# Score products with token slices as the stationary operand in an attention and mixture kernel

## The chip, the cores and the metric

One Trainium2 chip, one of its cores. The metric is the device time of one execution in microseconds (us). A run is one execution; the kernel before was timed in three, and one further execution was profiled. The engines are TensorE (PE in the profile; PEld is its weight load), VectorE (DVE), ScalarE (ACT), GpSimd (POOL) and SyncE (SP), which issues the large transfers. SBUF is the working memory of 128 partitions, PSUM the small memory of eight banks into which TensorE writes.

## What is computed

The agents attend to the keys, the queries attend to the agents, and the result x goes through a soft mixture of eight small networks with four slots each. There are 4 batches of 11456 tokens with 128 channels, 49 agents, and 32 slots in all. Everything is float32.

```python
def sm(a, b):                                   # softmax over b
    s = scale * (a @ b.transpose(0, 2, 1))
    e = np.exp(s - s.max(-1, keepdims=True))
    return e / (e.sum(-1, keepdims=True) + 1e-09)

agent_v = sm(agents, k) @ v                     # 4 x 49 x 128
x = (sm(q, agents) @ agent_v).reshape(45824, 128)

logits = x @ phi                                # 45824 x 32
d = softmax over the tokens (axis 0) of logits
c = softmax over the slots (axis 1) of logits
slot_input = d.T @ x                            # 32 x 128
slot_out[e] = np.maximum(slot_input[e] @ w1[e], 0.0) @ w2[e]
out = c @ slot_out
```

## The kernel before

**Tiling.** A batch has 90 cells of 128 tokens. A group is 16 cells (the last of a batch 10), so there are 24 groups of keys and 24 of queries. The x of the reference is never formed: the weights of the queries over the agents (`pt`) are multiplied with the agents' values times phi (`bd_m`), which gives the logits at once, and the sums over the tokens (`gp`) are taken of `pt`, too.

**Scores.** A batch is laid out as four streams of tokens (line 23). `scores` (line 227) makes four matmuls for each half h of the agents: the stationary operand is 32 agents (64 with padding), the moving one a stream's 512 tokens, and each stream's result goes to its own 32 partitions of a PSUM bank (tag "s", four banks). So the agents come out on partitions and the tokens along the row. Four matmuls with outputs on four strips of 32 partitions run side by side in the array; most float32 matmuls leave two records in the trace.

**Keys** (`k_ops`, line 239). `kx` and `kv` load a group; `ks` makes both halves of scores; `km` takes the maximum along the row (line 262); `kt`, `kr`, `kb`, `kn` carry the running maximum across the partitions through small matmuls into a bias per partition; `ke` (line 289) takes the exponential straight from PSUM with that bias. Then the tokens have to come to the partitions: `kT` transposes on VectorE in blocks of 32 x 32 (line 300), in group 0 on TensorE (`kP`, `kQ`). `kE` (line 318) multiplies with the values, two cells side by side on 64 partitions each; `kA` adds to the accumulator. At a batch's end `kg` and `kh` make `av` and `bd_m`.

**Queries** (`q_ops`, line 411). `qx` loads, `qs` makes scores, `qt` transposes them on VectorE into `pt` (line 434), `qm` takes the maximum over the 49 agents of each token (line 439). The exponential is made in one of two ways: for the even of the first 19 groups cell by cell on ScalarE with bias and accumulated sum (`qE`, line 460; `qw_act` on GpSimd), for the others with a subtraction on GpSimd (`qu`, line 444) and one exponential (`qe`, line 450; among the first 19 the sum is taken on VectorE, `qw_dve`, line 469). `qp` transposes `pt` on TensorE (line 504), `qc` copies it back, `ql` makes the logits: in the first 19 groups with the slots on partitions (line 481), which are transposed on VectorE (`qv`, line 490) and normalised on GpSimd (`qg`); in the last five with the tokens on partitions (line 517), normalised on VectorE (`qn`, lines 527 to 529). `qM` takes the column maximum over cells (line 536), `cr`, `cu`, `ce` the row softmax into `x_all`.

**Rounds** (`r_ops`, line 605). One or two groups make a round, 13 in all: `r1` to `r5` bring the column maximum to all partitions, `ru`, `re`, `rm` make the weighted exponentials `dt` (GpSimd, ScalarE, GpSimd; the multiplication of rounds 11 and 12 on VectorE, line 651), and `rg` sums `dt` x `pt` on TensorE (line 660: 32 columns stationary, 50 moving, four strips).

**End.** `z_` functions join the rounds and normalise, `m_` functions run the eight networks, `os`, `om`, `ot` (lines 872 to 889) normalise the first chunks of `x_all`, `fl` (line 891) are matmuls of no use to the result. The output loop (line 1016) makes 24 chunks with a matmul, two copies and a transfer each.

**Order.** Each engine runs its instructions in the order in which they are emitted. That order is the text `ORDER` (lines 47 to 104), which lists the steps of all groups interleaved; `_order` checks that each step stands behind what it needs, `_slots` gives the buffers in that order. `BUFS` (line 105) has the number of buffers: two `kt`, three `vt` and `qt`, four "s", three "a", one "m". The costs beside each step (`o("km", ..., 100 + 31 * n, ...)`) are notes for whoever makes the order; nothing on the chip reads them. The transfers of keys, values and queries all go through SP's queue, in the text's order, and each waits there for its buffer.

Of the kernel before, what the change touches and what calls it, by code (L numbers as in the profile page):

```python
# [16 lines left out]
S = E * SE  # L17
P = 128
# [7 lines left out]
NG = len(GROUPS)  # L26
EPS = 1e-9
# [20 lines left out]
qx qx qs.0 qs.1 qx qt.0 qs.0 qt.1 qm kx qs.1 qE.0 qt.0 qE.1 qs.0 qt.1 kv qm qs.1 qE.2 qt.0 qp.0  # L48
qu ks.0 qE.3 qt.1 ks.1 kx qm qe qp.1 km.0 qc.0 qp.0 qw@0 km.1 qc.1 qp.1 qc.0 qr kt qw@1 qE.0 kv
kr qr ks.0 qE.1 kb ks.1 km.0 kn ke.0 kx qp.0 km.1 ke.1 kP.0 qE.2 kt kr kb kT.0 kn ka kP.1 kx  # L50
qE.3 ks.0 kT.1 ke.0 ks.1 km.0 ke.1 kT.0 qp.1 kv qc.1 km.1 qw@2 qc.0 kE kT.1 qc.1 qr kx kt ks.0
kA kr kb kE km.0 kn ka ke.0 ke.1 kT.0 kv kT.1 ks.1 kA ks.0 km.1 kt kE km.0 kx kr kb kv ks.1 kA
kn ka ke.0 km.1 ke.1 ks.0 kT.0 kt ks.1 kr kT.1 kx kb kn km.0 ka kE ke.0 km.1 ke.1 kT.0 kT.1 kt
kv kr kE kA qx kb ks.0 kA kn ka ke.0 ks.1 ke.1 km.0 kT.0 km.1 kv kT.1 kt qs.0 kr kb kE qt.0 kn
ke.0 kx ke.1 kT.0 qs.1 kA kT.1 kg.2 qt.1 kg.1 kE kh.1 kh.2 qm kh.4 kv qu kg.3 kA ks.0 kh.3 ks.1
km.0 qe qx ql.0 km.1 ql.1 qn.0 kt ql.0 qn.1 kr qg ql.1 qn.0 kb kx qp.0 qn.1 kn ka qM qp.1 ke.0
qg qs.0 cr ke.1 qM cu qc.0 qs.1 qt.0 qc.1 ql.0 ce r1 kv qt.1 ql.1 qn.0 qm ks.0 kT.0 r2 qE.0
# [1052 lines left out]
```

## Time and profile before

| | us |
|---|---|
| three runs | 335.11, 337.64, 340.8 |
| median | 337.64 |
| the profiled execution | 333.75 |
| its span, first to last instruction | 332.0 |

The span is the time from the first to the last instruction of the profiled execution; the execution's own time is 1.75 us longer. Lines of the profile show, for an instruction or a group of them: the line of the kernel, the engine, the operation, what it writes and reads (tile names without buffer numbers), the shapes as partitions x elements, and a count. In the groups, the numbers behind the bar are busy time in us and the mean of one in ns, then the engine's idle time before them and what ended it. In the order of time, the first number is the start and the second the length in us. In the stretches, each engine has its busy us and its number of instructions, then come TensorE's granted clock, the busy share of the transfer engines and GB/s. Busy time of one engine can overlap at its ends, above all TensorE's, whose ends are modelled.

### The profile page before, as it was taken

The numbers are of one execution on the slowest core, as the hardware profiler recorded it, in microseconds if no ns is written. First come the engines' busy times: TensorE is split into PE (matmuls) and PEld (weight loads), VectorE is DVE, ScalarE is ACT, GpSimd is POOL, SyncE is SP. The second block draws the span as 40 slices with busy tenths as digits, with TensorE's granted clock in tenths as the row PEclk, the third lists the DMA queues.
The fourth block names the chain that finished last, engine by engine and source line by source line (L and its number), as shares of the span: only waits on it lengthen the run. The fifth ranks groups of instructions, "written<-read, shape, count | busy, mean of one in ns | idle before, by whom it ended". The sixth has DMA issues, their size and how long they took to land.

```text
span 332.0 us, 9455 instructions
## 1 busy us (share of the span) xinstructions
PE 274.5 (83%) x3821; PEld 152.7 (46%) x3821; DVE 264.7 (80%) x580; ACT 195.7 (59%) x613; POOL 139.8 (42%) x158
## 2 busy tenths in 40 slices
PE   1978978988998989898999989998978885866740
PEld 0234455544554455365556447467765551121210
DVE  0754675989998898999998988999949649998830
ACT  2496333484979685686956986374442246655540
POOL 0100001418382454638236938566886205343400
PEclk9999999999999999999999999999968999678555
DMA  7999899999979649989839990699400019999996
GB/s 298 423 409 359 319 395 418 421 410 402 393 275 397 216 135 423 411 340 358 360 121 424 360 400 5 218 408 424 176 0 2 2 77 415 423 414 422 410 424 265
DMA packets 15451, 104.18 MB, mean 314 GB/s; under 512 B 1840, under 2 KB 1968, under 8 KB 4016
## 3 DMA queue, kind: packets, MB, share of 16 engines
q1 hardware_dynamic: 14976, 102.95, 77.3%
q8 instruction: 30, 0.49, 0.6%
q10 hardware_dynamic: 432, 0.63, 0.5%
q14 instruction: 13, 0.11, 0.1%
HBM read 79.98 MB, written 23.59 MB: 312 GB/s over the span
## 4 chain that ended last, share of the span: by engine, by line
DVE 44%; PE 29%; DMA 11%; ACT 7%; POOL 4%; issue 3%; SPq 0%; ACTq 0%; DVEq 0%; POOLq 0%
PE ev L318 5%; DVE cm L536 5%; DMA out<-ot 5%; DVE pt L434 5%; PE sk L230 5%; PE sq L230 4%; ACT pt L460 3%; DVE mx L439 3%; DVE kmx L262 3%; DVE et L300 3%; DVE rm L541 3%; PE po L1025 3%; DMA qt<-qT 3%; DMA cs<-cst 3%; DVE row L274 3%
## 5 line engine op out<-in xcount | busy, mean ns | idle before, releaser
L460 ACT ACTIVATE pt<-pt,mx 128x49 f32<-128x49 f32 x160 | 51.4, 328 | 10.6 <-DVE mx L439 10.5
L230 PE MATMUL sq<-qt,ag 128*32 128x512 f32 (+1 forms) x384 | 48.1, 600 | 8.0 <-ACT ag L168 6.7
L1025 PE MATMUL po<-ct,sob 32*128 32x512 f32 (+1 forms) x192 | 35.4, 819 | 17.9 <-DVE ct L888 13.0
L230 PE MATMUL sk<-kt,ag 128*32 128x512 f32 (+1 forms) x384 | 46.9, 573 | 1.5 <-issue 0.9
L318 PE MATMUL ev<-vt,et 128*64 128x129 f32 x720 | 45.1, 276 | 3.3 <-DVE lt L490 1.4
L1030 ACT COPY ot<-po 128x1536 f32<-128x1536 f32 (+1 forms) x24 | 32.6, 1359 | 24.5 <-DVE ot L1029 24.5
L318 PEld LDWEIGHTS ev<-vt,et 128*64 128x64 f32 x720 | 39.3, 136 | 10.6 <-issue 2.3
L444 POOL TENSOR_TENSOR pt<-pt,mx 128x784 f32<-128x784 f32 (+1 forms) x14 | 19.3, 1378 | 57.6 <-DVE mx L439 55.6
L882 POOL TENSOR_TENSOR x_all<-x_all,cd 128x512 f32<-128x512 f32 (+1 forms) x24 | 23.9, 994 | 41.6 <-DVE cd L877 38.7
L262 DVE TENSOR_REDUCE kmx<-sk 128x1 f32<-128x512 f32 (+1 forms) x48 | 30.7, 641 | 9.2 <-PE sk L230 8.8
L544 POOL TENSOR_TENSOR x_all<-lt,rm 128x512 f32<-128x512 f32 (+1 forms) x24 | 24.2, 1015 | 25.3 <-DVE rm L541 21.4
L434 DVE STREAM_TRANSPOSE pt<-sq 128x512 f32<-128x512 f32 (+1 forms) x48 | 31.3, 660 | 4.1 <-PE sq L230 3.9
L511 ACT COPY pT<-tp 128x512 f32<-128x512 f32 (+1 forms) x48 | 25.4, 557 | 11.7 <-PE tp L504 11.5
L640 POOL TENSOR_TENSOR dt<-lt,mb 128x512 f32<-128x512 f32 (+1 forms) x24 | 28.7, 1212 | 7.4 <-ACT mb L634 7.1
L300 DVE STREAM_TRANSPOSE et<-es 128x512 f32<-128x512 f32 (+1 forms) x46 | 29.6, 650 | 1.9 <-ACT es L289 1.9
L460 ACT ACTIVATION_READ_ACCUMULATOR pt<-pt,mx 128x1 f32 x160 | 30.5, 191 | 0.0
L1025 PEld LDWEIGHTS po<-ct,sob 32*128 32x128 f32 x192 | 10.4, 240 | 42.5 <-ACT ot L1030 42.2
L289 ACT ACTIVATE es<-sk,nm 128x512 f32<-128x512 f32 (+1 forms) x48 | 29.3, 650 | 0.2
L495 POOL TENSOR_TENSOR lt<-lt,rt 128x512 f32<-128x512 f32 (+1 forms) x19 | 19.0, 999 | 23.0 <-DVE lt L490 22.9
L504 PE MATMUL tp<-cs,pt 128*128 128x128 f32 x180 | 27.2, 282 | 0.7 <-ACT pt L450 0.5
L504 PEld LDWEIGHTS tp<-cs,pt 128*128 128x128 f32 x180 | 19.3, 141 | 14.4 <-issue 4.2
L1029 DVE COPY ot<-po 128x512 f32<-128x512 f32 (+1 forms) x24 | 15.4, 643 | 12.6 <-DMA out<-ot 7.7
(123 smaller groups left out, 462.8 us busy)
## 6 DMA issues: line engine op xcount, KB each, us to landing
out<-ot SPq DMA_DIRECT2D x21, 1024.0 KB, 6.8
vt<-vL SPq DMA_DIRECT2D x20, 1032.0 KB, 10.0
qt<-qT SPq DMA_DIRECT2D x20, 1024.0 KB, 8.4
kt<-kT SPq DMA_DIRECT2D x20, 1024.0 KB, 7.0
w1s<-w SPq DMA_DIRECT2D x4, 1024.0 KB, 11.3
w2s<-w SPq DMA_DIRECT2D x4, 1024.0 KB, 12.0
vt<-vL SPq DMA_DIRECT2D x4, 645.0 KB, 8.4
kt<-kT SPq DMA_DIRECT2D x4, 640.0 KB, 7.5
```

Source lines behind the costliest of these rows:

```text
L230: t_.matmul(sp[32 * q4:32 * q4 + 32, :nt], ag[:, b, 32 * h:32 * h + 32], xv[:, q4, :], start=True, stop=True)
L262: v_.tensor_reduce(out=k["mx"][:, h:h + 1], in_=k["s"][h][:, :nt], axis=AX.X, op=ALU.max)
L289: s_.activation(out=k["e"][:, h, :nt], in_=k["s"][h][:, :nt], func=AF.Exp, bias=k["nm"][:, h:h + 1])
L300: v_.transpose(out=k["et"][:, :n, 32 * h:32 * h + 32], in_=k["e"][:, h, :nt].rearrange("p (t a) -> p t a", a=32))
L318: t_.matmul(k["ev"][o:o + 64, :], k["et"][:, c, :], k["v"][:, c, :], start=c < 2, stop=c >= n - 2)
L434: v_.transpose(out=q["pt"][:, :n, 32 * h:32 * h + 32], in_=q["s"][h][:, :nt].rearrange("p (t a) -> p t a", a=32))
L460: s_.activation(out=x, in_=x, func=AF.Exp, bias=q["mx"][:, c:c + 1], accum_out=q["dn"][:, c:c + 1])
L504: t_.transpose(q["tp", h][:, (c - h0) // 2, :], q["pt"][:, c:c + 2, :].rearrange("p c a -> p (c a)"), ident)
L511: s_.copy(out=q["pT"][:, h0 // 2:h1 // 2, :], in_=q["tp", h][:, :(h1 - h0) // 2, :])
L640: eng.tensor_tensor(out=q["dt"][:, :n], in0=q["lt"][:, :n, :], op=ALU.subtract, in1=r["mb"].unsqueeze(1).to_broadcast([P, n, S]))
L1025: t_.matmul(po[:, r, :32 * n], z["sob"][32 * r:32 * r + 32, :], z["ct", j][32 * r:32 * r + 32, :32 * n], start=True, stop=True)
L1030: s_.copy(out=ov[:, 1:4], in_=po[:, 1:4, :32 * n])
```

## The change

Both kinds of scores are made with the tokens on partitions. `scores` now takes 32 tokens as the stationary operand and the batch's 49 agents as the moving one: four matmuls a cell, one for each strip of 32 partitions, each 49 columns wide. The streams are gone from the layout of q, k and v; a cell is 128 tokens in a row.

For the keys, groups are 20 cells (four of 20 and one of 10 a batch, 20 in all; halves of 10 cells). `km` takes the maximum over cells for each agent, on each partition; `kt` turns it with four matmuls (`quad`), `kr`, `kb`, `kn` give a bias along the row, `ku` adds it on VectorE out of PSUM into `et`, `ke` takes the exponential there, and `kE` multiplies in four strips of 32 partitions. `kT`, `kP` and `kQ` go.

For the queries, `qm` reads the scores out of PSUM in two halves of eight cells; `qE` makes all exponentials cell by cell out of PSUM, without accumulated sums; the sum comes as one more column of `ql`, and `qn` (as in the last five groups before) normalises on VectorE for all groups. `qt`, `qu`, `qe`, `qw`, `qr`, `qL`, `qv`, `qg` go. `ql` makes four matmuls of 32 tokens for two cells.

In the rounds the maximum comes out on all 128 partitions, so that `rx`, `wr` and `ws` go; `rm` is on GpSimd in all rounds. The agents are scaled on VectorE instead of ScalarE, the constants shrink by 162 columns, the last entry of `FILL` goes from 7 to 2, and the memsets of setup go to GpSimd. `ORDER` is new from end to end: keys of the first batch first, `os` and `om` of chunks 1 to 5 before the last queries. The output loop is not touched.

```diff
-STREAMS = [(0, 2880), (2880, 2880), (5760, 2848), (8608, 2848)]
-QC = 16
+QC, KC = 16, 20
...
 ORDER = """
...
-qx qx qs.0 qs.1 qx qt.0 qs.0 qt.1 qm kx qs.1 qE.0 qt.0 qE.1 qs.0 qt.1 kv qm qs.1 qE.2 qt.0 qp.0
...
+kx@0 kx@1 ks.0 ks.1 kv@0 km.0 km.1 ks.1 ks.0 kx@2 kt km.0 kr km.1 kb kn ku.0 kt kv@2 ku.1
+ke.0@0 kr ke.1 kE.0@0 ka ks.0 kx@3 kE.1@0 km.0 ks.1 kA kb km.1 kn kv@1 ku.0 kt ku.1 ke.0@1 kr
...
-FILL = (0, 4, 4, 3, 4, 3, 7)
+FILL = (0, 4, 4, 3, 4, 3, 2)
...
-    s_.mul(out=ag, in_=ag, mul=SCALE)
+    v_.tensor_scalar(out=ag, in0=ag, scalar1=SCALE, scalar2=None, op0=ALU.mult)
...
+    ets = [kp.tile([P, KC, A2], F32, name=f"et{i}", tag=f"et{i}", bufs=1)
+           for i in range(BUFS["et"])]
+    for t in ets:
+        nc.gpsimd.memset(t[:, :, A:A2], 0.0)
...
-    def scores(b, xv, nt, h, nm):
-        sp = tile_("s", [P, 512], f"s{nm}")
-        for q4 in range(4):
-            t_.matmul(sp[32 * q4:32 * q4 + 32, :nt], ag[:, b, 32 * h:32 * h + 32],
-                      xv[:, q4, :], start=True, stop=True)
+    def scores(b, xt, c0, c1, nm):
+
+        sp = tile_("s", [P, c1 - c0, A], f"s{nm}")
+        for c in range(c0, c1):
+            for r in range(4):
+                t_.matmul(sp[32 * r:32 * r + 32, c - c0, :],
+                          xt[:, P * c + 32 * r:P * c + 32 * r + 32], ag[:, b, :],
+                          start=True, stop=True)
         return sp
 
+    def quad(out, lhs, rhs, **kw):
+
+        for r in range(4):
+            t_.matmul(out[32 * r:32 * r + 32], lhs(r), rhs, **kw)
+
...
         def km(h):
...
+            v_.tensor_reduce(out=o_, in_=sp.rearrange("p c a -> p a c"), axis=AX.X, op=ALU.max)
+            if h:
+                v_.tensor_tensor(out=mxs[i % 2][:, 0:A], in0=k["mx"][:, 0], in1=k["mx"][:, 1],
+                                 op=ALU.max)
...
+            quad(k["mt"], lambda r: mxs[i % 2][:, 32 * (r % 2):32 * (r % 2) + 32], ident,
+                 start=True, stop=True)
...
+            quad(k["mc"], lambda r: k["nm"].to_broadcast([P, 32]), ident[:, 0:A], start=True,
+                 stop=True)
...
+        def ku(h):
+            c0, c1 = cut[h]
             if h == 0:
...
+                k["e"] = ets[slots["et", now[0]].pop(0)]
+            v_.tensor_tensor(out=k["e"][:, c0:c1, 0:A], in0=k["s", h], op=ALU.add,
+                             in1=k["mb"].unsqueeze(1).to_broadcast([P, c1 - c0, A]))
+
+        def ke(h):
+            x = k["e"][:, cut[h][0]:cut[h][1], 0:A]
+            s_.activation(out=x, in_=x, func=AF.Exp)
+
+        def kE(h):
             if h == 0:
...
+                k["ev"] = tile_("a", [P, VC], f"ev_{i}")
+            for c in range(*cut[h]):
+                for r in range(2):
+                    o_ = 64 * (c % 2) + 32 * r
+                    t_.matmul(k["ev"][o_:o_ + 32, :], k["e"][:, c, 32 * r:32 * r + 32],
+                              k["v"][:, c, :], start=c < 2, stop=c >= n - 2)
...
+        def qm(h):
             if h == 0:
...
+                q["mx"] = sm.tile([P, QC], F32, name=f"mx_{i}", tag="mx")
+            v_.tensor_reduce(out=q["mx"][:, cut[h][0]:cut[h][1]], in_=q["s", h], axis=AX.X,
+                             op=ALU.max, negate=True)
+
+        def qz():
+            q["pt"] = tile_("pt", [P, QC, A1], f"pt_{i}")
+            nc.gpsimd.memset(q["pt"][:, :n, A], 0.0)
 
         def qE(h):
+            c0, c1 = cut[h]
+            for c in range(c0, c1):
+                s_.activation(out=q["pt"][:, c, 0:A], in_=q["s", h][:, c - c0, :], func=AF.Exp,
+                              bias=q["mx"][:, c:c + 1])
...
+        def ql(h):
+            c0, c1 = cut[h]
+            lp = q["lp", h] = tile_("a", [P, 8, S + 1], f"lp_{i}_{h}")
+            for c in range(c0, c1, 2):
+                for r_ in range(4):
+                    t_.matmul(lp[32 * r_:32 * r_ + 32, c - c0:c - c0 + 2, :],
+                              q["pT"][:, c // 2, 32 * r_:32 * r_ + 32], bd_m[b % 2],
                               start=True, stop=True)
...
         def qn(h):
...
+            v_.tensor_scalar(out=pt[:, c0:c1, A], in0=lp[:, :m, S], scalar1=EPS, scalar2=None,
+                             op0=ALU.add)
+            v_.reciprocal(out=rt[:, c0:c1], in_=pt[:, c0:c1, A])
+            v_.tensor_tensor(out=lt[:, c0:c1, :], in0=lp[:, :m, 0:S],
+                             in1=rt[:, c0:c1].unsqueeze(2).to_broadcast([P, m, S]), op=ALU.mult)
...
         def r2():
-            r["t1"] = tile_("m", [S, P], f"t1_{ri}")
-            t_.transpose(r["t1"], r["cmr"], ident)
+            r["t1"] = tile_("m", [P, P], f"t1_{ri}")
+            quad(r["t1"], lambda x: r["cmr"], ident, start=True, stop=True)
...
-        def rx():
-            r["mrep"] = sm.tile([S, P], F32, name=f"mrep_{ri}", tag="mrep", bufs=2)
-            s_.copy(out=r["mrep"], in_=m_all[:, ri:ri + 1].to_broadcast([S, P]))
...
-            eng = v_ if ri in MUL_DVE else nc.gpsimd
-            eng.tensor_tensor(out=dt, in0=dt, op=ALU.mult,
-                              in1=q["rt"][:, :n].unsqueeze(2).to_broadcast([P, n, S]))
+            nc.gpsimd.tensor_tensor(out=dt, in0=dt, op=ALU.mult,
+                                    in1=q["rt"][:, :n].unsqueeze(2).to_broadcast([P, n, S]))
```

More of the change, by code (lines that the diff above doesn't have):

```diff
@@ L52 @@
[L52 to L57, printed above, removed]
@@ L276, in kb @@
         def kb():
[L277 to L280 removed]
+            k["mc"] = tile_("m", [P, A], f"mc_{i}")
+            quad(k["mc"], lambda r: k["nm"].to_broadcast([P, 32]), ident[:, 0:A], start=True,
+                 stop=True)
         def kn():
[L283 removed]
@@ L396, in k_ops @@
-        ev = o("kE", (), "P", 133 * n, kE, deps=(t1_, v), takes=("a",),
-               gives=(("vt", v), ("et", t0_)))
+        x = o("kx", (), "D", 156 * n, kx, takes=("kt",))
+        v = o("kv", (), "D", 157 * n, kv_, takes=("vt",), deps=(x,))
+        hs_ = range(len(cut))
+        nh = [c1 - c0 for c0, c1 in cut]
+        s_h = [o("ks", (h,), "P", 107 * nh[h], lambda h=h: ks_(h), deps=(x,), takes=("s",),
+                 gives=(("kt", x),)) for h in hs_]
+        m = None
+        for h in hs_:
+            m = o("km", (h,), "V", 65 + 51 * nh[h] + (120 if h else 0) +
+                  (100 if last and cut[h][1] == n else 0), lambda h=h: km(h),
+                  deps=(s_h[h],) + ((m,) if m else ()))
@@ L507, in qc @@
-        def qc(h):
-            h0, h1 = half(h)
-            if h == 0:
-                q["pT"] = tile_("pT", [P, QC // 2, P], f"pT_{i}")
-            s_.copy(out=q["pT"][:, h0 // 2:h1 // 2, :], in_=q["tp", h][:, :(h1 - h0) // 2, :])
-        def ql(h):
-            h0, h1 = half(h)
-            lp = q["lp", h] = tile_("a", [P, 8, S + 1], f"lp_{i}_{h}")
-            for c in range(h0, h1, 2):
-                t_.matmul(lp[:, c - h0:c - h0 + 2, :], q["pT"][:, c // 2, :], bd_m[b % 2],
-                          start=True, stop=True)
+                q["mx"] = sm.tile([P, QC], F32, name=f"mx_{i}", tag="mx")
@@ new lines, in q_ops @@
+        for h in range(2):
+            cc.append(o("qc", (h,), "A", 45 + 54 * nh[h], lambda h=h: qc(h),
+                        deps=[ps_[h]] + cc[-1:], takes=() if h else ("pT",),
+                        gives=(("a", ps_[h]),)))
+        ls = []
+        for h in range(2):
+            ls.append(o("ql", (h,), "P", 55 * nh[h], lambda h=h: ql(h), deps=[cc[h], mm],
+                        takes=("a",), gives=(("pT", cc[0]),)))
+        for h in range(2):
+            nn.append(o("qn", (h,), "V", 240 + 37 * nh[h] + (80 if last and h else 0),
+                        lambda h=h: qn(h), deps=[ls[h], ps_[h]] + nn[-1:],
+                        takes=() if h else ("lt",), gives=(("a", ls[h]),)))
@@ L691, in r_ops @@
             o("rc", (), "A", 90, rc, deps=(f,), gives=(("a", ("rg", ri, 0)),))
-    for i in range(NT):
+    for i in range(NK):
         k_ops(i)
```

586 lines of the change are left out of this document (225 added, 361 removed).

## The prediction

> **What bounds the kernel now.** I read the page's busy times first, then the stretches by stage, then single groups of instructions, because an average over 332 us mixes three stages.
>
> ```profile
> span 332.0 us, 9455 instructions
> ...
> PE 274.5 (83%) x3821; PEld 152.7 (46%) x3821; DVE 264.7 (80%) x580; ACT 195.7 (59%) x613; POOL 139.8 (42%) x158
> ```
> ```profile
> core 0: us, PE busy (x) PEld busy (x) DVE busy (x) ACT busy (x) POOL busy (x), PEclk, DMA share, GB/s
> 0.00:10.00 10.00, 3.26 (x16) 0.74 (x20) 0.30 (x2) 1.70 (x2) 0.20 (x4) 1.00 0.84 320
> 10.00:60.00 50.00, 43.81 (x525) 22.71 (x517) 32.99 (x72) 27.31 (x104) 3.71 (x6) 1.00 0.98 387
> 60.00:241.00 181.00, 167.91 (x2734) 101.40 (x2727) 170.41 (x367) 126.01 (x463) 103.71 (x116) 1.00 0.81 320
> 241.00:269.00 28.00, 24.12 (x365) 17.50 (x365) 17.63 (x45) 8.04 (x21) 14.19 (x15) 0.88 0.01 2
> 269.00:332.00 63.00, 35.45 (x192) 10.36 (x192) 43.40 (x98) 32.62 (x24) 18.00 (x18) 0.71 0.91 375
> ```
> The main stage ends at 241 us, a tail of 28 us leads to the output stage of 63 us. Until 60 us the transfers run at 0.98 and VectorE is busy 33 of 50 us: loads set the pace. From 60 to 241 us VectorE is busy 170.4 of 181 us (94%). TensorE shows 167.9, but those ends are modelled and overlap, so its work has to be counted from the pace of its bursts:
>
> ```profile
> 192.32 0.92 PE L660 MATMUL gp<-pt,dt 128*32 128x50 f32 x64
> ...
> 198.98 1.09 PE L504 MATMUL tp<-cs,pt 128*128 128x128 f32 x8
> ...
> 206.61 1.99 PE L318 MATMUL ev<-vt,et 128*64 128x129 f32 x32
> 208.52 1.92 PE L230 MATMUL sq<-qt,ag 128*32 128x512 f32 x16
> ...
> 263.53 2.83 PE L857 MATMUL so_p<-w2s,ht 128*32 128x128 f32 x96
> ```
> ```profile
> L504 PE MATMUL tp<-cs,pt 128*128 128x128 f32 x180 | 27.2, 282 | 0.7 <-ACT pt L450 0.5
> ...
> L660 PE MATMUL gp<-pt,dt 128*32 128x50 f32 x720 | 12.3, 213 | 2.0 <-POOL dt L651 1.4 <-DVE acc L324 0.4 <-DVE dt L651 0.2
> ...
> L360 ACT ACTIVATE bd_m<-m,rm_a 128x32 f32<-128x32 f32 x8 | 1.9, 286 | 1.7 <-PE m L356 1.7
> ```
> Most of these matmuls leave two records a call. Scores cost 1.92 us for 16 cells, 0.120 us a cell and tensor, so 2 x 360 cells make 86 us. The value products (L318) start 1.91 us before what follows them: 0.119 a cell, 43 us. Transposes of pt: (1.09 - 0.28 of the last) / 7 = 0.116 us per two cells, 21 us. L660: without the 0.21 us of its last matmul, 0.71 us for 15 steps of four, 0.047 a step; 8.5 us in all. A step of four with 128 columns (L857) takes (2.83 - 0.27) / 23 = 0.111 us. The logits products (L481 in such steps, L517) are about 24 us, small ones some 15. TensorE holds about 198 us of work, VectorE 204 by the first three stretches. Two engines are nearly full, VectorE the fuller.
>
> **The change, part by part.**
>
> *VectorE.* The transposes of both scores, the row sums of L469 and the transposes of the logits go:
>
> ```profile
> L434 DVE STREAM_TRANSPOSE pt<-sq 128x512 f32<-128x512 f32 x40 | 27.3, 691 | 2.6 <-PE sq L230 2.5
> ...
> L262 DVE TENSOR_REDUCE kmx<-sk 128x1 f32<-128x512 f32 x40 | 26.8, 671 | 8.9 <-PE sk L230 8.8
> L300 DVE STREAM_TRANSPOSE et<-es 128x512 f32<-128x512 f32 x38 | 25.9, 686 | 1.9 <-ACT es L289 1.9
> ...
> L439 DVE TENSOR_REDUCE mx<-pt 128x16 f32<-128x784 f32 x20 | 19.1, 954 | 0.3
> ...
> L541 DVE TENSOR_REDUCE rm<-lt 128x16 f32<-128x512 f32 x20 | 13.2, 666 | 0.8 <-POOL lt L495 0.8
> ```
> ```profile
> 226.63 1.04 DVE L536 TENSOR_REDUCE cm<-lt 128x32 f32<-128x512 f32 x1
> 227.59 0.20 DVE L527 RECIPROCAL rt<-lp 128x8 f32<-128x8 f32 x1
> 227.70 0.12 DVE L528 COPY pt<-lp 128x8 f32<-128x8 f32 x1
> 227.83 0.42 DVE L529 TENSOR_TENSOR lt<-lp,rt 128x256 f32<-128x256 f32 x1
> 228.17 1.01 DVE L614 TENSOR_TENSOR cmr<-cm,cm 128x32 f32<-128x32 f32 x1
> ```
> What a group costs the queue is the distance to the next start: 0.96 us for L536, 0.58 for the three of L527 to L529, about 0.08 less than the mean for the others. After, 16 query cells cost: two maxima of 8 cells (half of L439's 784 elements each) 0.95, two halves of qn 1.16, qM 0.96, cr 0.59: 3.66, times 22.5 is 82 us. A key half of 10 cells: the add ku (490 elements beside 256 in 0.42, so about 0.65) and the maximum km. No row shows km, which steps over cells out of PSUM. L262 reads PSUM unstrided: 0.57 for 490 elements; L536 steps, out of SBUF: 0.92. I take 0.6, since PSUM is the source in L262, and keep 0.92 as the dear end. Over 36 halves ku and km are 45 us (57), the other key steps 14, round steps 6.5, head steps 8, five of the six `os` sums now inside the stage 5. Sum 161 us, 173 at the dear end, instead of 204.
>
> *TensorE.* A score cell is now four matmuls of 32 tokens by 49 columns in the four strips, eight records, two steps of four. L660 is that shape (32 stationary, 50 moving columns): 2 x 0.047 = 0.095 a cell, 68 us for 720 cells. The bounds: 0.089 (0.71 / 16, endless burst) and 0.115 (0.92 / 16, each burst alone), 64 to 83 us. kE in four strips of 129 columns: L857's step, 0.111 a cell, 40 us. ql with 66 columns lies between 0.047 and 0.111, by columns 0.060 a cell, 22 us. With 21, 8.5 and 15 as before: 175 us instead of 198, bounds 171 to 190. The program grows by some 6,500 matmul records; their issue is inside L660's pace.
>
> *ScalarE.* The exponentials of q lose their accumulator and read PSUM, now for all 24 groups; `qu`, `qe` and half of `qw` go.
>
> ```profile
> 191.09 0.33 ACT L460 ACTIVATE pt<-pt,mx 128x49 f32<-128x49 f32 x1
> ...
> 191.31 0.19 ACT L460 ACTIVATION_READ_ACCUMULATOR pt<-pt,mx 128x1 f32 x1
> 191.41 0.33 ACT L460 ACTIVATE pt<-pt,mx 128x49 f32<-128x49 f32 x1
> ...
> 216.91 0.47 ACT L360 ACTIVATE bd_m<-m,rm_a 128x32 f32<-128x32 f32 x2
> ```
> Two of L360 (PSUM in, a scale per partition) take 0.47 and one of them 0.286, so 0.18 start to start with 32 elements: about 0.20 with 49. Without the read the old form gives 0.22 (191.09 to 191.31). 360 x 0.20 = 72 us; the copies, ce, re, ke and small ones add about 84: 156 us (163 at 0.22), against 155 in the first three stretches. GpSimd loses qu and qg and stays below every other engine.
>
> *Loads and order.*
>
> ```profile
> vt<-vL SPq DMA_DIRECT2D x20, 1032.0 KB, 10.0
> qt<-qT SPq DMA_DIRECT2D x20, 1024.0 KB, 8.4
> kt<-kT SPq DMA_DIRECT2D x20, 1024.0 KB, 7.0
> ...
> cs<-cst ACTq DMA_DIRECT2D x1, 468.0 KB, 8.8
> ```
> ```profile
> 9.97 0.24 DVE L188 COPY bd_m<-cs 128x2 f32<-128x2 f32 x2 [8.84 <-DMA cs<-cst]
> ```
> Bytes stay 71 MB (three tensors of about 22.5 x 1 MB): 183 us at the early stage's 387 GB/s, so they can keep up with a stage of 200 us but not with one of 180. Keys now go first through SP's queue; kx waits behind two kt buffers, and a kx that waits holds the qx and kv issued after it. VectorE still can't begin before the constants land at about 10 us, with the agents' scaling ahead of that same wait; the smaller constants I price at nothing.
>
> *The stage.* The fullest engine of the old stage was busy 204 of 231 us (88%) from 10 us on. Now TensorE has 175, VectorE 161, ScalarE 156 and the loads 183 at the early pace, no one far ahead, so I take 86% for TensorE after 7 us of start: 7 + 175 / 0.86 = 210 us instead of 241.
>
> *The tail.* These rows stand on the way to the output:
>
> ```profile
> 248.94 2.65 DVE L651 TENSOR_TENSOR dt<-dt,rt 128x512 f32<-128x512 f32 x2
> ...
> 257.86 0.58 DVE L876 TENSOR_SCALAR cd<-cd 128x16 f32<-128x16 f32 x1
> 258.47 0.25 DVE L877 RECIPROCAL cd<-cd 128x16 f32<-128x16 f32 x1
> 258.64 0.63 DVE L834 TENSOR_SCALAR hs<-hp 128x512 f32<-128x512 f32 x1
> ...
> 267.17 1.56 PEld L894 LDWEIGHTS fl<-cs 128*128 128x128 f32 x14
> ```
> Two multiplications leave VectorE for GpSimd (2.65 us to about half: 1.3), most of the `cd` sums in front of the relu at 258.64 go earlier (about 1.5), two of the last seven fills go (4 of the 14 records in 1.56: 0.45); wr and ws go too, unpriced. 28 becomes about 24.5 us, and 28 if GpSimd is no sooner. The output stage is untouched: 63 us.
>
> **Sum** against the profiled execution: 210 + 24.5 + 63 = 297.5, and 1.75 us lie around its span (333.75 - 332.0): 299 us. The median shown, 337.64, is 1.2% above 333.75; on that scale, which all times below have, the forecast is 303 us.
>
> **Rivals.**
>
> *1. Slower: the small matmuls don't issue that fast.* There are 5,760 score records, so each further nanosecond is 5.8 us of TensorE. At 0.047 / 4 = 11.8 ns the sum holds; at 16.3 ns TensorE has 201 us and the stage is back at 241; from 18 ns the kernel is over 2% slower; at what a record of L857 costs (0.111 / 4 = 27.8 ns) TensorE has 267 us, the stage 317, the kernel 411 us. For it: bursts of L660 last under 1 us, and thousands in a row were never run. Against: 64 of that very shape in 0.92 us. 0.07. [...]
>
> *2. Smaller gain: the four `s` banks.* A key half now holds its bank until ku, behind km, kt, kr, kb, kn; a query half until the last of eight exponentials. 84 halves x hold / 4 banks: a mean hold of 7 us gives 147 us, hidden; 10 us gives 210, and with queue waits a stage of about 226. What queues behind: scores on TensorE, and through kt and qt the loads. 319 us. 0.20.
>
> *3. ScalarE becomes the bound* if 49 elements cost the old 0.32 (191.09 to 191.41): 199 us of work, 199 / 0.86 + 10 = 241, no gain in the stage, 334 us. The change then doesn't do what it says. 0.08.
>
> *4. A better fit:* TensorE reaches the 94% that VectorE has now: 7 + 175 / 0.94 = 193, kept from less by the loads; 286 us. 0.13.
>
> **How the numbers follow.** The forecast itself has 0.52, its own bounds (TensorE 171 to 190) give 299 to 321 us. Faster by over 2% (which a measurement of this kernel can about tell from no change): forecast, 2 and 4, 0.85; rival 3 is no change, 0.08; rival 1 slower, 0.07. The range of 284 to 324 us takes in 4 and 2 and leaves out 1 and 3.
>
> **What would show it.** Right: no STREAM_TRANSPOSE before the tail, VectorE under 175 us before it, bursts of scores at 0.095 us a cell, qE at 0.20 us start to start, the last cm near 210 us, the first output copy some 24 us later, output stage 63 us. Wrong: score bursts above 0.115 us a cell (1), TensorE idle on releases by ku or qE (2), ScalarE busy over 90% (3), or an output stage of another length.

## The result, and the profile after

The changed kernel took 461.75 us, the median of four runs (461.25 to 463.12), beside 336.38 us for the kernel before (four runs, 334.15 to 340.8). The ratio is 1.376, with a 95% interval from 1.367 to 1.386: 38% slower, where 303 us and a range of 284 to 324 were predicted. The profiled execution has a span of 460.4 us.

From the page of the changed kernel come the busy times, the granted clock over 40 slices, the queue that carries TensorE's instructions (packets, MB, share), and the chain that ended last:

```profile
span 460.4 us, 22881 instructions
...
PE 294.4 (64%) x10542; PEld 233.8 (51%) x10542; DVE 226.7 (49%) x572; ACT 193.3 (42%) x603; POOL 101.9 (22%) x129
...
PEclk9677787768898797989995897977778779988695
...
q8 instruction: 82, 1.34, 1.1%
...
PE 53%; issue 27%; DVE 8%; DMA 7%; ACT 2%; DVEq 0%; SPq 0%; ACTq 0%
```

No engine is busy for two thirds of the span, and 27% of the chain is "issue": time in which an engine waited for nothing that the profile shows. The row of q8 says what to look at. It counts 82 packets and 1.34 MB, so 16 KB a packet. TensorE ran 10,542 matmuls and as many weight loads, 21,084 instructions, and 21,084 / 82 is 257: a packet is a block of about 256 instructions, some 64 bytes each. The page of the kernel before has the same row with 30 packets, one in 11 us:

```profile
q8 instruction: 30, 0.49, 0.6%
```

By stage, in the stretches of the changed kernel (start to the last `cm`, to the first output copy, to the end):

```profile
core 0: us, PE busy (x) PEld busy (x) DVE busy (x) ACT busy (x) POOL busy (x), PEclk, DMA share, GB/s
10.00:376.00 366.00, 237.55 (x9849) 206.22 (x9838) 171.66 (x443) 151.96 (x561) 74.24 (x91) 0.82 0.56 213
376.00:399.00 23.00, 22.38 (x403) 16.04 (x401) 11.57 (x32) 7.50 (x18) 8.35 (x10) 0.96 0.01 2
399.00:461.00 62.00, 31.86 (x184) 8.88 (x176) 43.22 (x98) 32.59 (x24) 17.98 (x18) 0.77 0.92 381
```

The whole loss lies in the main stage: it ends at 376 us instead of 241. Tail and output stage take 23 and 62 us. In the main stage VectorE has 171.7 us of work, well under the old 204, and ScalarE 152 beside 155; both wait for TensorE, which is itself idle for 35% of the stage. What TensorE waits for, from its waits (us in total, times, longest):

```profile
PE sk L240 <- issue: 34.3, 15, 4.2
PE sq L240 <- issue: 32.1, 18, 5.0
PE gp L606 <- issue: 18.1, 6, 5.1
PE lp L481 <- issue: 15.3, 6, 5.2
PE ev L335 <- issue: 15.1, 8, 4.4
...
PE sk L240 <- DVE ag L174: 7.3, 1, 7.3
```

These five rows make 115 us of "issue" in pieces of up to 5 us. They fall on the stage's main kinds of matmul, and after the start and before the output stage TensorE hardly waits for another engine. The kernel before has one piece of this kind among its scores:

```profile
PE sk L230 <- issue: 0.9, 1, 0.9
```

TensorE's timeline of the changed kernel (start, us, engine, line, records, idle before) shows how such a piece looks:

```profile
134.74 0.62 PE L240 MATMUL sq<-ag,qt 128*32 128x49 f32 x34
139.54 0.78 PE L240 MATMUL sq<-ag,qt 128*32 128x49 f32 x26 [4.18 <-issue]
...
140.32 3.28 PE L335 MATMUL ev<-vt,et 128*32 128x129 f32 x77
143.36 1.07 PE L240 MATMUL sk<-ag,kt 128*32 128x49 f32 x79
```

In the middle of one group's scores, with operands and banks there, nothing starts for 4.2 us. Then 26 records come at (0.78 - 0.28) / 25 = 20 ns, with the granted clock at 0.50, and at 143.36, with the clock at 1.00, 79 records take 1.07 us: less 0.2 for the last one 11 ns a record and 0.089 us a cell, the pace that was predicted. Over the main stage the starts of successive score records in a burst lie 11.6 ns apart at the full clock (3,788 of them) and 20.5 ns at the halved one (1,676). So at the full clock the records are as fast as forecast while they come, and at times they don't come.

Three costs of the prediction, two of them priced without a row of their own (`km` and the exponentials), stand as follows, from the groups of the changed kernel on VectorE and the timelines of ScalarE and TensorE:

```profile
L286 DVE TENSOR_REDUCE kmx<-sk 128x49 f32<-128x490 f32 x32 | 20.7, 664 | 42.6 <-PE sk L240 40.9 <-PE t L248 1.7
```
```profile
181.54 1.66 ACT L460 ACTIVATE pt<-sq,mx 128x49 f32<-128x49 f32 x8
```
```profile
183.62 2.40 PE L335 MATMUL ev<-vt,et 128*32 128x129 f32 x78
```

`km` takes 0.66 us by itself (about 0.58 on the queue, by the prediction's 0.08; 0.6 was taken), an exponential 1.66 / 8 = 0.21 us (0.20), kE (2.40 - 0.28) / 77 x 4 = 0.110 us a cell (0.111).

### The profile page after: what moved, and what is told of

Same layout as the page of the kernel before. It is cut to its first block, busy times and chain, and to the rows that moved or that the text cites. A ratio compares the mean times of both kernels' runs of the same rounds, so it can differ in the third digit from the quotient of the medians.

```text
span 460.4 us, 22881 instructions
## 1 busy us (share of the span) xinstructions
PE 294.4 (64%) x10542; PEld 233.8 (51%) x10542; DVE 226.7 (49%) x572; ACT 193.3 (42%) x603; POOL 101.9 (22%) x129
## 3 DMA queue, kind: packets, MB, share of 16 engines
q8 instruction: 82, 1.34, 1.1%
## 4 chain that ended last, share of the span: by engine, by line
PE 53%; issue 27%; DVE 8%; DMA 7%; ACT 2%; DVEq 0%; SPq 0%; ACTq 0%
PE sq L240 10%; PE ev L335 9%; PE sk L240 9%; PE tp L468 7%; PE lp L481 6%; DMA out<-ot 5%; PE gp L606 2%; DMA kt<-kT 2%; PE po L954 2%; PE t L248 1%; DVE ot L958 1%; PE mt L248 1%; PE fl L825 1%; ACT ot L959 1%; DVE ct L819 1%
## 5 line engine op out<-in xcount | busy, mean ns | idle before, releaser
L460 ACT ACTIVATE pt<-sq,mx 128x49 f32<-128x49 f32 x360 | 74.3, 330 | 23.1 <-DVE mx L450 23.0
L240 PE MATMUL sk<-ag,kt 128*32 128x49 f32 x2880 | 52.9, 238 | 41.8 <-issue 34.3
L240 PE MATMUL sq<-ag,qt 128*32 128x49 f32 x2880 | 54.9, 230 | 32.1 <-issue 32.1
L240 PEld LDWEIGHTS sk<-ag,kt 128*32 128x32 f32 x2880 | 47.8, 132 | 45.4 <-issue 37.1
L240 PEld LDWEIGHTS sq<-ag,qt 128*32 128x32 f32 x2880 | 47.1, 126 | 40.6 <-issue 39.5
L335 PE MATMUL ev<-vt,et 128*32 128x129 f32 x1440 | 56.1, 303 | 15.6 <-issue 15.1
L335 PEld LDWEIGHTS ev<-vt,et 128*32 128x32 f32 x1440 | 47.4, 123 | 19.7 <-issue 18.2
L481 PE MATMUL lp<-bd_m,pT 100*32 100x66 f32 x1440 | 38.4, 254 | 16.5 <-issue 15.3
L481 PEld LDWEIGHTS lp<-bd_m,pT 100*32 100x32 f32 x1440 | 31.9, 131 | 19.3 <-issue 16.6
L468 PE MATMUL tp<-cs,pt 128*100 128x128 f32 x180 | 35.8, 343 | 0.7 <-DVE lt L495 0.7
```

What stands on the lines that cost most here:

```text
L240: t_.matmul(sp[32 * r:32 * r + 32, c - c0, :], xt[:, P * c + 32 * r:P * c + 32 * r + 32], ag[:, b, :], start=True, stop=True)
L335: t_.matmul(k["ev"][o_:o_ + 32, :], k["e"][:, c, 32 * r:32 * r + 32], k["v"][:, c, :], start=c < 2, stop=c >= n - 2)
L460: s_.activation(out=q["pt"][:, c, 0:A], in_=q["s", h][:, c - c0, :], func=AF.Exp, bias=q["mx"][:, c:c + 1])
L468: t_.transpose(q["tp", h][:, (c - c0) // 2, :], x[:, A1 * c:A1 * c + AP2], ident)
L481: t_.matmul(lp[32 * r_:32 * r_ + 32, c - c0:c - c0 + 2, :], q["pT"][:, c // 2, 32 * r_:32 * r_ + 32], bd_m[b % 2], start=True, stop=True)
```

## The experiments

Three theories stood against each other. **T1**: TensorE's instructions come in blocks of 256, the next block is asked for too late, and short matmuls drain a block faster than the next one comes. **T2**: the array, PSUM or the fallen clock is slow for small strips. **T3**: the new order, its buffers and its waits cost the time. The times of the kernel before on the same chips were 337.67 us beside the first four kernels, 340.35 beside the next three, and 335.67 beside the last three.

### The kernel before, with each score matmul cut into pieces of 64 columns

```diff
-            t_.matmul(sp[32 * q4:32 * q4 + 32, :nt], ag[:, b, 32 * h:32 * h + 32],
-                      xv[:, q4, :], start=True, stop=True)
+        for t in range(0, nt, 64):
+            for q4 in range(4):
+                t_.matmul(sp[32 * q4:32 * q4 + 32, t:t + 64], ag[:, b, 32 * h:32 * h + 32],
+                          xv[:, q4, t:t + 64], start=True, stop=True)
```

> The kernel before, unchanged in order, layout and results, except that each score matmul of 512 moving tokens (L230) is issued as eight of 64: 768 score records become 6144, TensorE's instructions rise from about 7,600 to about 18,400, the array's cycles stay. Theory T1 (TensorE's instructions arrive in blocks of 256, the next block is only asked for when the one before is entered, and 128 matmuls with their weight loads drain faster than a block comes): 72 blocks at 4 to 5.5 us with 140 us of other array-bound time gives 390 to 430 us, and the waits of TensorE show idle of the kind 'issue' at L230 of 50 us or more. Theory T2 (short strip matmuls as such are slow in the array or at the PSUM write): about the same 390 to 430 us, but as a longer busy time of the score records and no 'issue' idle. Theory T3 (the new layout, the new order and its waits made the changed kernel slow, not its number of instructions): 335 to 350 us.

Measured: 439.23 us, where the kernel before took 337.67; that is 9 us over what T1 gave. The score records became 5,760, not 6,144, because the last group of a batch needs only five pieces. Its page has 69 packets on q8, and the waits of TensorE read

```profile
PE sk L231 <- issue: 29.4, 13, 3.9
PE sq L231 <- issue: 22.0, 12, 4.0
PE lq L482 <- issue: 11.8, 4, 5.0
```

The old kernel, in its old order and layout, with the same columns to move and only more instructions, becomes slow in the same way. T3 isn't needed for this. Of the 101 us that were lost, 70 are "issue" in all its rows, as T1 said; TensorE's busy time rose by 51 us (274.5 to 325.6). In bursts without a stop the cut records aren't longer than their share of the old ones: 40 of them take 0.77 us at 174.72, (0.77 - 0.21) / 39 = 14 ns, where an eighth of the old 120 ns is 15. The 58 that come after a stop of 3.09 us, at 182.68, take 1.91 us, 33 ns each over the whole burst, where the 40 take 19.

### Scores as one matmul a cell

```diff
-            for r in range(4):
-                t_.matmul(sp[32 * r:32 * r + 32, c - c0, :],
-                          xt[:, P * c + 32 * r:P * c + 32 * r + 32], ag[:, b, :],
-                          start=True, stop=True)
+            t_.matmul(sp[:, c - c0, :], xt[:, P * c:P * c + P], ag[:, b, :],
+                      start=True, stop=True)
```

> The changed kernel with the scores of a cell (L240) as one matmul with all 128 tokens stationary in place of four strips of 32: 4,320 matmul records and as many weight loads less, 33.8 of 82 blocks, but each cell now takes the array about 0.22 us where four strips side by side took 0.095 us, so TensorE's own work grows by some 95 us. T1 (instruction supply): about 49 blocks, faster than the changed kernel, 370 to 410 us. T2 (the array's own pace): slower than the changed kernel, 500 to 555 us. T3 (order and waits): 460 us or more.

Measured: 458.83 us, beside 461.75 for the changed kernel. The time misses what T1 gave, but the time has changed its kind. The page, and the largest "issue" row of its waits:

```profile
PE 403.5 (88%) x6222; PEld 347.4 (76%) x6222; DVE 228.4 (50%) x572; ACT 194.5 (43%) x603; POOL 101.7 (22%) x129
...
q8 instruction: 49, 0.80, 0.7%
```
```profile
PE sq L239 <- issue: 4.0, 2, 3.0
```

TensorE's busy time rose from 294.4 to 403.5 us (109 us, where I had reckoned 95 from 0.22 us a cell, an estimate of mine with no row behind it; at 161.67 the 16 records of eight cells take 1.88 us, (1.88 - 0.3) / 15 x 2 = 0.21 us a cell), and the "issue" idle of 115 us is down to about 7 in all its rows. The one paid for the other. My 370 to 410 us had counted blocks without adding all of the array's work; T2's 500 us had added the work without taking the idle away. By its time alone the run would fit T3, which gave 460 us or more; the waits tell them apart, since TensorE is now busy and doesn't wait for other engines.

### kE alone in two strips of 64

```diff
-                for r in range(2):
-                    o_ = 64 * (c % 2) + 32 * r
-                    t_.matmul(k["ev"][o_:o_ + 32, :], k["e"][:, c, 32 * r:32 * r + 32],
-                              k["v"][:, c, :], start=c < 2, stop=c >= n - 2)
+                o_ = 64 * (c % 2)
+                t_.matmul(k["ev"][o_:o_ + 64, :], k["e"][:, c, :],
+                          k["v"][:, c, :], start=c < 2, stop=c >= n - 2)
```

> The changed kernel with kE (L335) in two strips of 64 stationary columns in place of four of 32: 720 matmul records and 720 weight loads less, that is 5.6 blocks of 256 instructions of some 82; the array's work of kE rises, as every record still streams the same moving columns but fewer strips run side by side. T1 (instruction supply): 5.6 blocks at 3.5 to 5 us less, 433 to 442 us. T2 (the array or the clock): no change or up to 10 us slower, 460 to 470 us. T3 (order and waits): 455 to 465 us.

Measured: 457.69 us, 4 us less with five blocks less. This is a miss for T1 as I had put it, which gave 433 to 442; the time alone lies in T3's range (455 to 465). A reading that fits: a record of kE moves 129 columns and costs 27.5 ns by the row at 183.62, so 128 of them take 3.5 us, hardly less than a block needs to come (3.7 us, below). In strips of 64 half as many records take about twice as long each (55 ns in the run with all strips at 64, 20 records in 1.32 us at 167.88), TensorE's busy time rises by 10 us (294.4 to 304.2), and so the blocks that go saved little waiting. No run isolates this.

### The scores alone in two strips of 64

```diff
-            for r in range(4):
-                t_.matmul(sp[32 * r:32 * r + 32, c - c0, :],
-                          xt[:, P * c + 32 * r:P * c + 32 * r + 32], ag[:, b, :],
+            for r in range(2):
+                t_.matmul(sp[64 * r:64 * r + 64, c - c0, :],
+                          xt[:, P * c + 64 * r:P * c + 64 * r + 64], ag[:, b, :],
                           start=True, stop=True)
```

> The changed kernel with the scores alone (L240) in two strips of 64 tokens in place of four of 32; kE, ql and the rest stay in strips of 32. Some 5,760 of TensorE's 21,100 instructions go, 22.5 of 82 blocks. T1 (instruction supply), with what the run with kE in strips of 64 showed: a record that moves 129 columns keeps the array busy about as long as its share of a block takes to come, so taking kE's records away saves nothing, while the scores' records of 49 columns drain in under half of that; then nearly all of the gain of the run with all strips at 64 comes from the scores: 355 to 385 us. If blocks cost the same whatever is in them, 22.5 of the 35 blocks that that run saved give 22.5/35 of its 115 us: 388 us. T2 and T3 (array, order): 440 us or more.

Measured: 388.49 us with 60 packets on q8. The scores by themselves give back 73 us, 3.3 us a block. That is the figure of equal blocks (388), not the 355 to 385 that I had made of the run with kE; the reading given there is at most part of the matter.

### All strips at 64

The scores and kE as above, ql in two matmuls of 64, `kt` in two, `kb` and `r4` in one each:

```diff
-            quad(k["mc"], lambda r: k["nm"].to_broadcast([P, 32]), ident[:, 0:A], start=True,
-                 stop=True)
+            t_.matmul(k["mc"], k["nm"].to_broadcast([P, P]), ident[:, 0:A], start=True, stop=True)
...
-                for r_ in range(4):
-                    t_.matmul(lp[32 * r_:32 * r_ + 32, c - c0:c - c0 + 2, :],
-                              q["pT"][:, c // 2, 32 * r_:32 * r_ + 32], bd_m[b % 2],
+                for r_ in range(2):
+                    t_.matmul(lp[64 * r_:64 * r_ + 64, c - c0:c - c0 + 2, :],
+                              q["pT"][:, c // 2, 64 * r_:64 * r_ + 64], bd_m[b % 2],
```

> The changed kernel with scores (L240), kE (L335) and the ql matmuls (L481) in strips of 64 stationary columns in place of 32, the km transposes (kt) in two matmuls, and the two broadcasts of the running maximum (kb and r4) as one matmul each: some 5,900 instead of 10,500 matmul records, 47 blocks instead of 82; same order, same buffers, same waits, same work on VectorE and ScalarE; the array's own work rises to about 190 to 200 us. T1 (instruction supply): 320 to 350 us, and the idle of TensorE put down to 'issue' falls from some 115 us to under 30. T2 (array pace, or the lower clock): 440 to 480 us. T3 (order and waits): 440 us or more, the idle going over to releases by other engines.

Measured: 346.62 us, the median of four runs, where T1 gave 320 to 350; against the kernel before 1.028, interval 1.020 to 1.036. Of the 125 us that the change lost, 115 are back, with the order, the buffers, the waits and all work of the other engines as in the changed kernel. T2 and T3 had 440 us and more. Its page, and its main stage from 60 us to the last `cm`:

```profile
PE 284.3 (83%) x5944; PEld 229.5 (67%) x5944; DVE 227.3 (66%) x572; ACT 192.3 (56%) x603; POOL 101.7 (30%) x129
...
q8 instruction: 47, 0.77, 0.9%
```
```profile
60.00:258.00 198.00, 180.68 (x4387) 160.78 (x4386) 143.89 (x377) 132.56 (x497) 72.26 (x89) 0.97 0.75 290
```

Now TensorE's own work is the bound: 180.7 of 198 us (91%). Its timeline has the scores of eight cells as

```profile
106.81 1.14 PE L240 MATMUL sq<-ag,qt 128*64 128x49 f32 x32
```

Less 0.2 us for the last record these are 0.94 us for 31, so 30 ns a record and 0.12 us a cell of four records, where strips of 32 take 0.09 to 0.10 while instructions come.

### TensorE alone

```diff
+    scores(32 * 16)
+    wait(big)
+    for x in range(56):
+        b, o = x // 5 % 4, 2048 * (x % 5)
+        nc.sync.dma_start(out=big[x % 4], in_=qT[b, :, o:o + 2048])
+    scores(32 * 22)
+    wait(big + few)
+    for x in range(224):
+        b, o = x // 20 % 4, 512 * (x % 20)
+        nc.sync.dma_start(out=few[x % 16], in_=kT[b, :, o:o + 512])
+    scores(32 * 22)
+    wait(few)
+    wide(32 * 8)
+    scores(32 * 12, 8)
```

`scores` issues the loop of L240 on one resident tile, `wide` the same with 196 moving columns, and the second argument cuts the moving columns.

> Not the reference's computation: five stretches of matmuls on TensorE alone, with no other engine beside it, on tiles that are there already; the output is filled with one tile. Stretch 1: 2,048 matmuls of the changed kernel's score form (32 stationary columns, 49 moving, four strips), no transfers: 16 blocks of 256 instructions. Stretch 2: 2,816 of them (22 blocks) while SP loads 56 MB in packets of 8 KB. Stretch 3: the same 2,816 while SP loads 56 MB in packets of 2 KB. Stretch 4: 1,024 matmuls (8 blocks) of 196 moving columns. Stretch 5: 1,536 matmuls (12 blocks) of 8 moving columns, no transfers. The array's own pace by the bursts of the changed kernel is 24 ns a matmul of 49 columns. T1 (blocks of 256 instructions, asked for one at a time, at least 3.4 us each, and later when transfers stand in front): stretch 1 about 55 us (3.4 us a block), stretch 2 about 130 to 150 us (6 to 7 us a block), stretch 5 about 41 us (3.4 us a block, for a sixth of the columns), stretch 4 by the array, 100 us. If transfers delay the fetch by the length of the packets in front of it, stretch 3 is 80 to 100 us; if by their bytes, as stretch 2. T2 (the array or PSUM): stretches 1 to 3 alike per matmul, 50 us, 68 us, 68 us, and stretch 5 far below stretch 1.

Measured: 767.41 us. I had counted calls, and a call leaves two matmul and two weight load records, so every stretch is twice as long as I wrote: 32, 44, 44, 16 and 24 blocks, and q8 has 160. The figures a block are not touched by that. The transfers of stretch 3 also began late and ran on into stretch 4, so windows of time are read in place of stretches: without transfers, with packets of 8 KB, without, with packets of 2 KB, with 196 columns beside those, and with 8 columns.

```profile
20.00:120.00 100.00, 50.70 (x3403) 46.52 (x3394) 0.00 (x0) 0.00 (x0) 0.85 0.02 4
140.00:260.00 120.00, 53.17 (x2532) 49.61 (x2536) 0.00 (x0) 0.00 (x0) 0.62 1.01 417
300.00:440.00 140.00, 70.46 (x4844) 64.73 (x4834) 0.00 (x0) 0.00 (x0) 0.88 0.02 4
470.00:515.00 45.00, 20.01 (x1024) 18.53 (x1024) 0.00 (x0) 0.00 (x0) 0.70 1.03 374
550.00:605.00 55.00, 55.00 (x1331) 44.95 (x1327) 0.00 (x0) 0.00 (x0) 1.00 1.04 378
620.00:700.00 80.00, 41.86 (x2843) 39.89 (x2833) 2.27 (x4) 0.00 (x0) 0.55 0.02 5
```

The columns are the busy times (with records) of PE, PEld, DVE and POOL, then clock, DMA share and GB/s. Matmuls and weight loads of a row over 256 are its blocks: 26.6 in 100 us, 3.8 us a block without transfers; 19.8 in 120, 6.1 us beside packets of 8 KB; 37.8 in 140, 3.7 us without; 8 in 45, 5.6 us beside packets of 2 KB (5.4 by the starts of the blocks, which the ends of a window don't disturb); 22.2 in 80, 3.6 us for 8 columns. The timeline shows the blocks themselves:

```profile
63.41 1.59 PE L182 MATMUL sp<-ag,xt 128*32 128x49 f32 x128 [2.14 <-issue]
67.41 1.78 PE L182 MATMUL sp<-ag,xt 128*32 128x49 f32 x128 [2.41 <-issue]
...
202.79 2.70 PE L182 MATMUL sp<-ag,xt 128*32 128x49 f32 x128 [3.36 <-issue]
208.98 2.84 PE L182 MATMUL sp<-ag,xt 128*32 128x49 f32 x128 [3.50 <-issue]
...
559.71 15.61 PE L189 MATMUL lp<-ag,xt 128*32 128x196 f32 x370
...
664.44 1.90 PE L182 MATMUL sp<-ag,xt 128*32 128x8 f32 x128 [1.85 <-issue]
667.91 1.89 PE L182 MATMUL sp<-ag,xt 128*32 128x8 f32 x128 [1.58 <-issue]
```

No other engine works beside TensorE, no operand is awaited, and yet after exactly 128 matmuls (256 instructions) it stands still, for 1.6 to 3.5 us in these rows and up to 4.6 in the whole run (141 stops of the kind "issue", 313.5 us). Eight columns take as long a block as 49, so the columns don't set it; 196 columns keep the array busy for 5.3 us a block (10.4 blocks in 55 us), about as long as a block takes to come beside packets of 2 KB, and the stop is gone (TensorE is busy for 55.0 of the 55 us). This is T1, with two prices: 3.7 us a block, and 6.1 us beside transfers of 8 KB packets.

The trace of this run also keeps the times of the packets on q8, and they show where a block's time goes (medians). Without transfers the next block's packet starts 1.1 us after the first instruction of the block before, takes 1.0 to 1.1 us, and 1.4 us after its end the stop is over: some 3.6 us together. Beside packets of 8 KB it starts only 3.7 us after that first instruction, beside 2 KB 2.8 us after; its length and the 1.4 us stay. So transfers delay the start of the packet and hardly lengthen it. The main stage of the changed kernel agrees: of the stops that end so, the next packet starts 1.15 us after the first instruction where the transfer engines are under 10% busy (20 stops) and 3.7 us after it where they are over 90% busy (19; medians).

### The changed kernel without its loads

```diff
+    once = {}
+
     def load(tag, src, b, ca, cb, most):
+        if tag in once:
+            return once[tag]
...
+        once[tag] = xt
         return xt
...
         def kv_():
-            k["v"] = tile_("vt", [P, KC, VC], f"vt_{i}")
+            if "vt" in once:
+                k["v"] = once["vt"]
+                return
+            once["vt"] = k["v"] = tile_("vt", [P, KC, VC], f"vt_{i}")
```

> The changed kernel without its key, value and query loads after the first of each kind: every group computes on the first group's tile, so the output is not the reference's; all instructions of TensorE, VectorE, ScalarE and GpSimd stay, in the same order. T1 (instruction supply, which transfers delay): some 71 blocks of the main stage at 3.4 to 3.6 us, 245 to 260 us, with the tail and the output stage 345 to 365 us; TensorE still shows idle put down to 'issue', but less of it, and bursts still end at block bounds. If the fetch has its length whatever the transfers do, 430 to 460 us. T3 (order and waits, with loads late): no 'issue' idle at all and 300 us or less; T2 (array and clock): 440 to 460 us.

Measured: 402.11 us, 60 us under the changed kernel and 37 to 57 over what T1 had given. From 14 to 278 us:

```profile
14.00:278.00 264.00, 180.80 (x8793) 158.22 (x8794) 146.13 (x369) 130.14 (x476) 55.16 (x72) 0.95 0.04 12
```

(8,793 + 8,794) / 256 is 68.7 blocks in 264 us, 3.84 us each: I had taken 3.4 to 3.6, the least distance between two blocks, where TensorE alone has 3.7 to 3.8. So of the loss about 60 us go with the transfers, beside which a block comes late, and the rest is there with hardly a transfer running. T3's 300 us is excluded: with no data to wait for, the stage still goes at the pace of the blocks.

### Loads in packets of 2 KB

```diff
-        nc.sync.dma_start(out=xt[:, :P * (cb - ca)], in_=src[b, :, P * ca:P * cb])
+        for c in range(ca, cb, 4):
+            e = min(c + 4, cb)
+            nc.sync.dma_start(out=xt[:, P * (c - ca):P * (e - ca)], in_=src[b, :, P * c:P * e])
```

The value loads are cut in the same way.

> The changed kernel with each key, value and query load cut into pieces of four cells, so that a packet carries 2 KB instead of 8 to 10 KB; the same bytes on the same queue, some 220 issues on SP in place of 44, everything else as it was. If a block of instructions waits behind the packets that are queued on its DMA engine by number (some eight of 0.39 us each), shorter packets let it through sooner: 4 us instead of 6 to 7 us a block beside transfers, 370 to 410 us. If it waits behind a number of bytes, or if the transfers are not what delays it, no change: 450 to 465 us.

Measured: 458.74 us, no gain to speak of. Beside packets of 2 KB a block still took 5.4 to 5.6 us in the run of TensorE alone, and transfers run for longer (a share of 0.64 of the main stage in place of 0.56). Shorter packets are no cure. The same cut of the loads, made in the kernel with all strips at 64:

> The kernel with all strips at 64, and each key, value and query load cut into pieces of four cells (packets of 2 KB). Beside transfers a block took 6.1 us with packets of 8 KB and some 5.4 us with 2 KB; of this kernel's 47 blocks some 30 come while transfers run, but most of them are spaced by the array's work (5 to 6 us). If the instruction supply beside transfers is what still holds it: 325 to 340 us. If it is bound by TensorE's own work (busy 83% of the span, 91% in the main stage): 340 to 350 us, no difference that can be measured.

Measured: 340.84 us; against the kernel before 1.011, interval 0.999 to 1.024. This is the changed kernel's best form here with exact scores, and no difference from the kernel before is shown: TensorE is busy for 55 to 57 of every 60 us from 60 to 240 us.

### The rest of the change, with TensorE out of the way

```diff
+            x = xt[:, P * c:P * c + P].bitcast(mybir.dt.bfloat16).rearrange("p (t x) -> p x t", x=2)
+            a = ag[:, b, :].bitcast(mybir.dt.bfloat16).rearrange("p (t x) -> p x t", x=2)
+            t_.matmul(sp[:, c - c0, :], x[:, 1], a[:, 1], start=True, stop=True)
```

> The kernel with all strips at 64, and the scores of a cell as one matmul of 128 tokens on the upper 16 bits of each number (bf16 views of the same tiles), so the scores are less exact than the reference's: one record a cell in place of four, some 3,800 matmul records in all and 30 blocks, as many as the kernel before, and TensorE's own work some 60 us less. VectorE, ScalarE, GpSimd, loads, buffers and order are those of the changed kernel. It asks what the rest of the change is worth once TensorE neither waits for instructions nor is the bound. If the rest of the forecast holds (VectorE 161 to 173 us in a stage of 210 us), 295 to 315 us. If the new order with four score banks or its waits cost time of their own (T3), 335 us or more. In between, the array's work that is left or the loads decide.

Measured: 310.6 us, span 308.8, beside 335.67 us for the kernel before.

```profile
10.00:60.00 50.00, 39.85 (x546) 33.14 (x546) 30.62 (x76) 21.65 (x75) 1.12 (x2) 0.86 1.01 419
60.00:130.00 70.00, 57.33 (x1085) 48.55 (x1083) 58.02 (x149) 51.20 (x190) 25.85 (x33) 0.92 0.99 402
130.00:224.00 94.00, 77.09 (x1579) 63.15 (x1579) 81.88 (x219) 76.85 (x297) 46.37 (x56) 0.95 0.79 298
224.00:247.00 23.00, 21.12 (x389) 15.20 (x392) 12.50 (x31) 7.16 (x18) 8.92 (x10) 1.00 0.01 2
247.00:309.00 62.00, 33.83 (x188) 9.24 (x180) 43.69 (x98) 32.62 (x24) 18.00 (x18) 0.73 0.92 381
```

With 29 packets on q8 (30 before) and less TensorE work, the same order, banks and waits give a main stage of 224 us (210 forecast), a tail of 23 (24.5) and an output stage of 62 (63). T3 is out. What is left over the forecast seems to lie in the first 130 us, where the transfers run at 0.99 to 1.01 and VectorE is busy 74% of the time from 10 us on, 87% after it. Most likely the loads set the pace there, where the forecast had TensorE at 86%; no run shows it.

## Why the prediction was wrong

**The step that failed** is in the part on TensorE: "The program grows by some 6,500 matmul records; their issue is inside L660's pace." The growth is right (6,721), and at the full clock so is the pace in a burst. But L660's row is 64 records long, less than the 128 of a block, and says nothing of the stop that comes after each block when blocks are short of work. The sum took 198 us of array work down to 175 and let the instructions come for nothing; in the main stage they took 119.6 us of stops (below).

**What it cost, worked out.** The row of the main stage from 10 to 376 us has 9,849 + 9,838 instructions, 76.9 blocks, and transfers for 0.56 of the time. With the two prices of the run of TensorE alone, 76.9 / (0.56 / 6.1 + 0.44 / 3.7) = 365 us; it took 366. That the two meet to 1 us is partly luck, since the share is a mean over the transfer engines. The packets of q8 in the trace show the same directly: in the main stage there are 78, 4.7 us apart on average. Of 65 pieces of over 0.3 us in which TensorE runs neither a matmul nor a weight load, 55, with 119.6 of 126.3 us, end 1.15 to 1.65 us after the end of such a packet, about 255 instructions or a multiple of that after the one before. In the kernel before 2 of 22 such pieces do, 1.5 us. The blocks of the kernel before come 11 us apart on average (8.5 from 60 to 241 us), far above either price, and there the supply is hidden.

**The rivals.** The outcome is on the side of rival 1, which had 0.07: the small matmuls don't issue that fast. Its doubt ("thousands in a row were never run") was the right one. Its dearest price was what a record of L857 costs (27.8 ns, 411 us), whereas the mean over the main stage is 366 us / 9,849 = 37 ns a record of any kind. The sign named for it, score bursts above 0.115 us a cell, was met where the clock was halved (20.5 ns a record on average, 0.16 us a cell, under a third of the records); the others stayed at 0.093, since the loss lies mainly between bursts. The sign to look for was the "issue" in TensorE's waits, which no step had named. So the rival had the direction and the doubt right and the mechanism wrong: its prices are all of the pace within a burst. Rivals 2 to 4 played no part: TensorE hardly waits for another engine, ScalarE is busy for 42% of the stage, and the fit is no better than taken.

**What was right.** VectorE's work up to the last `cm` is 172 us, within the 161 to 173 given, at its dear end though `km` took the cheap one; ScalarE's is 152 (156 forecast); kE, the exponentials and `km` cost what was said. The tail and the output stage are a little better than forecast. The run with light scores shows these terms together, though with other work on TensorE: 310.6 us for a forecast of 303.

**The clock** isn't what sets the time of a block here. It is 0.82 in the main stage of the changed kernel, but in the run of TensorE alone it is 0.55 to 0.88 in the stretches with stops and 1.00 in the one without, and a block of 8 columns at 0.55 comes in 3.6 us, no later than one of 49 at 0.88. The changed kernel without its loads goes at 3.84 us a block with the clock at 0.95. What the lowered clock adds to the 125 us by slowing the bursts isn't separated.

**What stays open.** Why the packet of the next block starts 1.7 to 2.6 us later beside transfers isn't settled: shorter packets brought a block from 6.1 to 5.4 us only. That kE in wider strips gave 4 us where its five blocks at 3.3 would be 16 is explained by a reading that no run isolates.

## What to carry to other kernels

Count TensorE's instructions before splitting a matmul into narrow strips: a call in fp32 here is four of them (two matmuls, two weight loads), and by these runs a block of 256 costs about 3.7 us, some 6 beside heavy transfers, so 64 such calls with less array work than that don't run any faster. Read the count of instruction packets on the page and divide: at 11 us a block the supply was hidden, at 4.8 it was the bound. A pace read from a burst shorter than a block doesn't hold for a stage of such bursts.

## What the runs showed of the hardware

- A block of 256 TensorE instructions takes 3.6 to 3.8 us to come with nothing else running, whether its matmuls move 8 or 49 columns, 6.1 us beside transfers at 417 GB/s in 8 KB packets, and 5.4 to 5.6 us beside 2 KB packets at 374 GB/s. The delay lies before the block's packet starts; the packet itself takes 1.0 to 1.1 us in all three.
- In the run of TensorE alone the granted clock was 0.62 at 6.1 us a block, 0.70 at 5.4 to 5.6 us, 0.85 at 3.8 us and 0.55 at 3.6 us with 8 columns, all with stops, and 1.00 where 196 columns fill the block's time.
- Scores in fp32 cost the array somewhat more in two strips of 64 than in four of 32 (0.12 us a cell beside 0.09 at the full clock), while one matmul of 128 tokens made TensorE's busy time grow by 109 us over 720 cells.
